# Four chunks turned by VectorE and by DMAs through memory instead of by TensorE, in a two-layer attention and SwiGLU kernel

## The chip, the cores and the metric

The kernel runs on one core of one Trainium2 chip. The metric is the device time of one execution in microseconds (us); the median of the runs counts. Engines are named as in the profile: PE is TensorE, DVE is VectorE, ACT is ScalarE, POOL is GpSimd, SP is SyncE, whose queue issues nearly all transfers here.

## The reference

Two layers of the same two blocks, with the same weights in both, on x of 2048 rows by 448 in float32:

```python
x = x + A(layernorm(x))   # 16 heads of 28; one key and one value head for all
x = x + B(layernorm(x))   # (silu(x @ w_gate) * (x @ w_up)) @ w_down, inner width 1792
x = x + A(layernorm(x))
x = x + B(layernorm(x))

q = (x @ wq) by heads; k = x @ wk; v = x @ wv
A = softmax(q k^T * 28**-0.5) v, heads side by side, @ wo
```

## The kernel before

The 2048 rows are four chunks of 512, numbered c = 0 to 3 in the code and 1 to 4 in the text. A chunk is four tiles of 128 rows by 448. The residual `xres` stays in SBUF. A product needs the normalized chunk turned, with the 448 features on the partitions: four blocks of 128, the last of which holds 64 features twice. `flipped` makes from each turned block a rounded high part `xh` (a ScalarE copy) and a low part `xl` (a VectorE subtraction); of the fourth block the low part lies in the upper half of `xh`, and in the feed-forward the high part of the upper half in `xd`.

There are two ways from rows to a turned chunk, and `norm_steps(c, away)` prepares for either: statistics (`stat`), the scale (`scale`, on POOL), and then for each of four tiles `apply`, which normalizes.

- With `away` false the tiles go to `xn`, and `flip` has TensorE transpose them, 16 transposes of 128x128 into four PSUM banks (line 275), from which `flipped` reads.
- With `away` true each tile is normalized into `sg` (of which there is one buffer, that the feed-forward's SiLU writes too), VectorE transposes it in blocks of 32x32 (`turn`, line 239), and `send` writes the blocks to a tensor `xt` in memory with four DMAs (line 248). `load` brings it back as `raw` with two DMAs (lines 128 and 129), and `cut` calls `flipped` on that. Line 129 reads the last 64 rows and writes them twice, to both halves of the partitions.

The order on each engine's queue is the order in which the program is written down; nothing is reordered. Each engine takes its queue in order and waits at an instruction until its data and buffers are ready.

The stages of a layer are the projections of q, k and v (`Attention.project`, 16 calls, four for each chunk), the scores with softmax and p v, and the feed-forward. The feed-forward goes through the inner width in seven groups of two blocks, and in each group through the four chunks; one block of one chunk is a `unit`. A unit writes in this order: the first half of its gate and up products, the first half of the down product of the unit before, the second half of its own, the second half of the other, and then SiLU, product and rounding of `h`. Between the halves ScalarE copies one column of each bank that was written (`between`, `seen`, line 328); TensorE's next write to that bank comes after that copy.

Work is hung on units by counters: an entry `[n, f]` of `soon` runs at the end of a unit, when its counter, lowered once a unit, is below zero; `mid[gi, c, n]` runs in the middle of that unit; `plan[n, z]` runs in the n-th call of `project`, before (z = 0) or after (z = 1) its product.

- Layer 1's projections turn all four chunks on TensorE. The chunks 1 to 3 that go into the feed-forwards are turned by VectorE and DMAs during the scores.
- Chunk 4 of the feed-forward (`rest`) is normalized at the second unit, and TensorE transposes it in `mid[0, 2, 1]`, two units before the first that multiplies it.
- Layer 2's projections begin inside layer 1's last group (`hand_over(c)`, called when chunk c has got its last addition). Chunk 1 is turned by VectorE and DMAs; chunks 2, 3 and 4 by TensorE, each one call of `project` before the first that needs it (`project` looks ahead in `order`, where the first of a chunk has m = 3).

The first three calls of `project` of layer 2 run at the end of the last unit, the fourth after it, then `flush` (the last down product and its additions), and `finish` runs the other twelve. Each call has ScalarE copy its product from the bank to `stage` (two buffers here) and SP store that to `qd` and `kt`.

Weights of the feed-forward lie in `wgh` and `wgl`, three buffers each (`FG + 1`). During the hand-over these also serve as buffers for `vt`, `wrq` and `q2`.

Of the kernel before, what the change touches and what calls it, by code (L numbers as in the profile page):

```python
# [8 lines left out]
F32 = mybir.dt.float32  # L9
F32R = mybir.dt.float32r  # L10
# [5 lines left out]
P = 128  # L16
# [10 lines left out]
FG = 2  # L27
# [25 lines left out]
def forward(  # L53
# [14 lines left out]
    nc = tc.nc  # L68
# [9 lines left out]
    pers = ctx.enter_context(tc.tile_pool(name="pers", bufs=1))  # L78
    ps = ctx.enter_context(tc.tile_pool(name="ps", bufs=1, space=PSUM))
    dram = ctx.enter_context(tc.tile_pool(name="dram", bufs=1, space=bass.MemoryType.DRAM))  # L80
    wpool = ctx.enter_context(tc.tile_pool(name="wpool", bufs=1))
# [3 lines left out]
    phase, banks, threes, live, turn = ExitStack(), [], [], set(), {}  # L85
# [40 lines left out]
    def rows3(dst, src):  # L126
        n = src.shape[1]
        nc.sync.dma_start(dst[:, 0:3], src[0:384, :].rearrange("(k p) n -> p k n", p=P))
        nc.sync.dma_start(dst[:, 3], src[384:448, :][None].to_broadcast([2, 64, n]))
# [83 lines left out]
    def norm_steps(c, away=False):  # L213


        got = {}
        cs = slice(4 * c, 4 * c + 4)

        def stat(t):
            nc.vector.bn_stats(stats[:, 4 * c + t, :], xres[:, 4 * c + t, :])  # L220
            nc.vector.bn_aggr(mv[:, 4 * c + t, :], stats[:, 4 * c + t, :])

        def scale():
            rstd = pers.tile([P, 4], F32, name="rstd", bufs=2)
            nc.gpsimd.tensor_scalar(rstd, mv[:, cs, 1], 1.0, EPS, ALU.mult, ALU.add)
            nc.gpsimd.tensor_tensor(rstd, rstd, halfn, ALU.pow)
            got["r"] = rstd

        def apply(t):
            if t == 0:  # L230
                got["x"] = pers.tile([P, 4, 512], F32, name="xn")
            got["o"] = (pers.tile([P, 512], F32, name="sg") if away else got["x"][:, t, :])[:, 0:D]
            i, r = xres[:, 4 * c + t, :], got["r"][:, t : t + 1]
            nc.vector.tensor_scalar(got["o"], i, mv[:, 4 * c + t, 0:1], r, ALU.subtract, ALU.mult)
            if not away:
                nc.gpsimd.tensor_copy(got["x"][:, t, D:512], got["o"][:, 384:D])

        def turn(t):
            nc.vector.transpose(side()[:, :, :, t], got["o"].rearrange("p (k s) -> p k s", s=32))

        def side():
            return got["x"].rearrange("p t n -> p (t n)")[:, 0 : 4 * D].rearrange("p (k s t) -> p k s t", s=32, t=4)

        def send():
            turns.append(dram.tile([D, 512], F32, name=f"xt{len(turns)}"))
            got["xt"] = turns[-1]
            for a in range(4):
                nc.sync.dma_start(
                    got["xt"].rearrange("(k r) n -> r k n", r=32)[:, :, P * a : P * a + P],
                    side()[32 * a : 32 * a + 32].rearrange("p k s t -> p k (s t)"),  # L250
                )

        def load():
            got["raw"] = pers.tile([P, 4, 512], F32, name="xn")
            rows3(got["raw"], got["xt"])

        got["load"] = load
        fs = [lambda t=t: stat(t) for t in range(4)] + [scale]
        for t in range(4):
            fs += [lambda t=t: apply(t)] + [lambda t=t: turn(t)] * away  # L260
        return fs + [send] * away, got
# [3 lines left out]
    def cut(got, tiles, ks=range(4), copy=nc.scalar.copy):  # L265

        for k in ks:
            flipped(tiles, k, got["raw"][:, k, :], copy)

    def flip(got, tiles, ks=range(4)):  # L270

        for k in ks:
            pt = bank(wide[-1])[1]
            for t in range(4):
                nc.tensor.transpose(in_turn(pt)[:, t, :], got["x"][:, t, P * k : P * k + P], ident)  # L275
            flipped(tiles, k, pt, nc.scalar.copy)

    def flipped(tiles, k, pt, copy, steps=(0, 1)):

        xh, xl, xd = tiles  # L280
        twice = xd if k == 3 else None
        if 0 in steps and twice is None:
            copy(xh[:, k, :], pt)
        elif 0 in steps:
            copy(xh[0:64, k, :], pt[0:64, :])
            copy(xd[64:128, :], pt[64:128, :])
        if 1 in steps and k < 3:
            nc.vector.tensor_tensor(xl[:, k, :], pt, xh[:, k, :], ALU.subtract)
        elif 1 in steps:
            high = xh[64:128, k, :] if twice is None else xd[64:128, :]  # L290
            nc.vector.tensor_tensor(xh[64:128, k, :], pt[64:128, :], high, ALU.subtract)
# [31 lines left out]
    seen = pers.tile([P, 4], F32, name="seen")  # L323
# [8 lines left out]
    class Attention:  # L332
# [232 lines left out]
        def scores(self, ff):  # L565
            next(switch)
            with tc.tile_pool(name=f"at{self.layer}", bufs=1, reuse_waits="tile") as wp:
# [126 lines left out]
                for c in range(3):  # L694
                    ff.X[c] = xtile(xpool) if c < 2 else None
                    fs, got = norm_steps(c, True)
                    n = NT * (4 * c + 5)
                    for kt, f in enumerate(fs):
                        later[n + kt] = f
                    later[n + 22] = got["load"]  # L700
                    for k in range(4) if c < 2 else ():
                        for z in range(2):
                            later[n + 34 + 2 * k + z] = lambda c=c, got=got, k=k, z=z: flipped(
                                ff.X[c], k, got["raw"][:, k, :], nc.vector.tensor_copy, (z,)
                            )
                ff.norms[2] = got
                last = NT * len(GR)
# [43 lines left out]
    class FeedForward:  # L751
# [68 lines left out]
        def hand_over(self, c):  # L820

            a = self.nxt
            fs, got = norm_steps(c, c == 0)
            for f in fs[:5]:
                f()
            a.pool = self.stage
            a.X[c] = xtile(xpool if c < 2 else self.xbp)

            def ready():
                for f in fs[5:]:  # L830
                    f()
                a.norms[c] = got

            if c == 0:
                self.soon.append([1, lambda: [f() for f in fs[5:]]])
                self.soon.append([2, got["load"]])
                self.soon.append([4, lambda: cut(got, a.X[c])])
                self.soon.append([5, lambda: [a.project() for _ in range(3)]])
            elif c == 1:
                self.soon.append([2, ready])  # L840
            else:
                a.plan[4 * c - 4, 0] = [ready]

        def turned(self, c, ks=range(4)):
            flip(self.norms[c], self.X[c], ks)

        def flush(self):

# [69 lines left out]
        def rest(self, xb):  # L918
            self.stage = xb.enter_context(tc.tile_pool(name=f"stage{self.layer}", bufs=2, reuse_waits="tile"))
            self.xbp = xb.enter_context(tc.tile_pool(name=f"xb{self.layer + 1}", bufs=2, reuse_waits="tile"))  # L920
            xd = xb.enter_context(tc.tile_pool(name=f"xd{self.layer}", bufs=1, reuse_waits="tile"))
            self.xd = [xd.tile([P, 512], F32R, name=f"xd{c}") for c in range(NC)]
            for c in (0, 1):
                dma(self.xd[c][64:128, :], self.X[c][0][0:64, 3, :])
                self.X[c] = (*self.X[c][:2], self.xd[c])
            for c in (2, 3):
                self.X[c] = xtile(self.xbp, self.xd[c])
            cut(self.norms[2], self.X[2])
            third, self.norms[3] = norm_steps(3)
            for f in third[:5]:  # L930
                f()
            self.soon.append([1, lambda: [f() for f in third[5:]]])
            self.mid[0, 2, 1] = [lambda ks=ks: self.turned(3, ks) for ks in ((0, 1), (2, 3))]
            for gi, fs in enumerate(groups):
                if self.layer == 1 and fine is not None and gi in (2, 3):
                    self.verdict(gi == 3)
                    if gi == 3:
                        tc.mark_branch_hint_location("again", engines=(ET.Activation, ET.DVE, ET.Pool, ET.SP, ET.PE))
                for c in range(NC):
                    for n in range(len(fs)):  # L940
                        if gi or c:
                            self.unit(gi, c, n)
                if gi == len(groups) - 2 and self.nxt:
                    self.nxt.w = load_wqkv(xb.enter_context(tc.tile_pool(name="wqkv1", bufs=1, reuse_waits="tile")), None)[1]
            if self.nxt:
                self.nxt.project()
            self.flush()
# [11 lines left out]
    fs, got = norm_steps(0)  # L959
# [28 lines left out]
    for c in range(1, NC):  # L988
        fs, got = norm_steps(c)
# [39 lines left out]
```

## Time and profile before

| | |
|---|---|
| median of 3 runs | 1986.07 us (1986.04 to 1986.16) |
| profiled execution, span | 1984.8 us |
| between the span and the median | 1.3 us |
| PE busy | 1969.2 us (99%) |
| ACT busy | 1278.6 us (64%) |
| DVE busy | 812.1 us (41%) |
| POOL busy | 528.7 us (27%) |
| transposes of line 275 | 144 |
| DMA, mean | 39 GB/s |

Of the profiled execution the page gives the span, from its first instruction to its last; the runs' time is taken around it. A line of a timeline has the start in us from the span's start, the duration, engine and line, what was written from what, the count of instructions run together, and in brackets the idle time before and what ended it. In the chain, which merges pieces, a line is start, duration, engine, tile and line. Lines of waits end with the total, the count and the longest.

### The profile page before, as it was taken

The numbers are of one execution on the slowest core, as the hardware profiler recorded it, in microseconds if no ns is written. First come the engines' busy times: TensorE is split into PE (matmuls) and PEld (weight loads), VectorE is DVE, ScalarE is ACT, GpSimd is POOL, SyncE is SP. The second block draws the span as 40 slices with busy tenths as digits, with TensorE's granted clock in tenths as the row PEclk, the third lists the DMA queues.
The fourth block names the chain that finished last, engine by engine and source line by source line (L and its number), as shares of the span: only waits on it lengthen the run. The fifth ranks groups of instructions, "written<-read, shape, count | busy, mean of one in ns | idle before, by whom it ended". The sixth has DMA issues, their size and how long they took to land. (4 is left out here: it accounts for less than half of the span.)

```text
span 1984.8 us, 44687 instructions
## 1 busy us (share of the span) xinstructions
PE 1969.2 (99%) x18519; PEld 1322.9 (67%) x18519; DVE 812.1 (41%) x1410; ACT 1278.6 (64%) x2140; POOL 528.7 (27%) x571
## 2 busy tenths in 40 slices
PE   9999999999999999999999999999999999999998
PEld 7544545445458999999984444454454789988887
DVE  7444543544434222322554335445454432222222
ACT  4899797997953333333349998979979433333332
POOL 4212111132213233333341221111231232233320
PEclk9999999999999999999999999999999999999999
DMA  5101020121210011100131111102111101011102
GB/s 163 55 23 31 23 51 21 32 58 28 72 33 9 24 32 32 32 24 19 51 107 35 30 31 30 44 12 61 32 55 45 31 17 30 18 31 32 32 1 76
DMA packets 93382, 77.52 MB, mean 39 GB/s; under 512 B 23510, under 2 KB 76374, under 8 KB 93174
## 3 DMA queue, kind: packets, MB, share of 16 engines
q1 hardware_dynamic: 92886, 74.16, 13.5%
q8 instruction: 146, 2.39, 0.5%
q14 instruction: 62, 0.51, 0.1%
q10 hardware_dynamic: 288, 0.46, 0.1%
HBM read 55.06 MB, written 18.74 MB: 37 GB/s over the span
## 5 line engine op out<-in xcount | busy, mean ns | idle before, releaser
L647 PE MATMUL bank<-pt,vsb 128*32 128x512 f32 x4096 | 493.3, 598 | 0.5
L604 PE MATMUL bank<-qstack,keys 32*128 32x512 f32 x1536 | 484.2, 424 | 1.7 <-DVE xres L591 1.7
L604 PE MATMUL three<-qstack,keys 32*128 32x512 f32 x4608 | 461.4, 425 | 1.5 <-DVE vt L538 1.2
L604 PEld LDWEIGHTS three<-qstack,keys 32*128 32x128 f32 x4608 | 254.2, 182 | 295.0 <-ACT pt L617 181.1
L321 PE MATMUL bank<-xh,wgh 64*128 64x512 f32 x1728 | 437.5, 389 | 0.1
L611 ACT ACTIVATE pt<-three 128x1536 f32<-128x1536 f32 x256 | 372.2, 1454 | 0.6 <-ACT pt L617 0.3
L617 ACT ACTIVATE pt<-three 128x1536 f32<-128x1536 f32 x256 | 372.0, 1453 | 0.0
L321 PE MATMUL bank<-xh,wgl 64*128 64x512 f32 x1404 | 363.0, 390 | 0.0
L321 PE MATMUL bank<-wdh,h 64*128 64x448 f32 x1792 | 330.2, 364 | 1.4 <-ACT h L889 1.0
L321 PE MATMUL bank<-xl,wgh 64*128 64x512 f32 x1296 | 328.3, 389 | 0.0
L888 DVE TENSOR_TENSOR sg<-bank,sg 128x512 f32<-128x512 f32 x112 | 77.4, 691 | 497.6 <-ACT sg L887 488.4
L647 PEld LDWEIGHTS bank<-pt,vsb 128*32 128x32 f32 x4096 | 107.1, 109 | 250.2 <-issue 152.6
L613 DVE COPY raw<-bank 128x512 f32<-128x512 f32 x256 | 177.2, 692 | 230.7 <-PE bank L604 228.5
L321 PEld LDWEIGHTS bank<-xh,wgh 64*128 64x128 f32 x1728 | 256.9, 184 | 16.7 <-issue 0.9
L798 POOL TENSOR_TENSOR xres<-stage,xres 128x448 f32<-128x448 f32 x108 | 127.7, 1203 | 499.6 <-ACT stage L797 499.6
L657 DVE TENSOR_TENSOR o<-bank,o 128x512 f32<-128x512 f32 x224 | 154.9, 691 | 241.7 <-PE bank L647 237.1
L321 PEld LDWEIGHTS bank<-wdh,h 64*128 64x128 f32 x1792 | 240.5, 184 | 15.6 <-issue 2.0
L604 PEld LDWEIGHTS bank<-qstack,keys 32*128 32x128 f32 x1536 | 243.8, 183 | 4.6 <-DVE xres L591 3.6
L328 ACT COPY seen<-bank 128x1 f32<-128x1 f32 x664 | 81.0, 163 | 238.9 <-PE bank L321 236.4
L321 PEld LDWEIGHTS bank<-xh,wgl 64*128 64x128 f32 x1404 | 212.1, 184 | 13.8
L321 PE MATMUL bank<-wdl,h 64*128 64x448 f32 x896 | 215.6, 367 | 0.0
L887 ACT ACTIVATE sg<-bank 128x512 f32<-128x512 f32 x112 | 67.3, 601 | 223.2 <-PE bank L321 214.2
(127 smaller groups left out, 2259.3 us busy)
## 6 DMA issues: line engine op xcount, KB each, us to landing
o<-rd SPq DMA_DIRECT2D x32, 256.0 KB
qraw<-qd SPq DMA_DIRECT2D x128, 56.0 KB
qd<-stage SPq DMA_DIRECT2D x30, 224.0 KB
xt<-xn SPq DMA_DIRECT2D x28, 224.0 KB
wdr<-in_B_w_down_dram SPq DMA_DIRECT2D x28, 224.0 KB
xn<-xt SPq DMA_DIRECT2D x7, 768.0 KB
wr<-in_B_w_gate_dram SPq DMA_DIRECT2D x28, 192.0 KB
wr<-in_B_w_up_dram SPq DMA_DIRECT2D x28, 192.0 KB
```

The costliest lines, as they stand in the source:

```text
L321: nc.tensor.matmul(po, a, b, start=start, stop=stop, skip_group_check=True)
L328: nc.scalar.copy(seen[:, i : i + 1], po[:, 0:1])
L604: nc.tensor.matmul(three[:, j, :] if j < 3 else one, k[js, kp, ks], q[js, part, :], start=(z == 0), stop=(z == 2), tile_position=(32 * j, 0),)
L611: nc.scalar.activation(pt, three, AF.Exp, scale=SCALE)
L613: nc.vector.tensor_copy(raw, one)
L617: nc.scalar.activation(pt, three, AF.Exp, scale=SCALE)
L647: nc.tensor.matmul(po[32 * j : 32 * j + 32, :], vsb[:, n % NT, :], pts[n][j], start=(n == 2 * d), stop=(n > 2 * d), skip_group_check=True,)
L657: nc.vector.tensor_tensor(acc, in_turn(po), acc, ALU.add)
L798: nc.gpsimd.tensor_tensor(r, s, r, ALU.add)
L887: nc.scalar.activation(by_tile(sg), in_turn(pg[0]), AF.Silu)
L888: nc.vector.tensor_tensor(by_tile(sg), in_turn(pg[1]), by_tile(sg), ALU.mult)
```

## The change

Chunk 4 of both feed-forwards and chunks 2 to 4 of layer 2's projections go the way of `away=True`. Their transposes on TensorE and the POOL copies that belong to them are gone; for each, VectorE makes four block transposes, SP issues four stores to memory and the loads back, and ScalarE and VectorE cut the parts from SBUF instead of PSUM. `load` has a second form that reads into two buffers taken from the weights' tags, with three DMAs (new lines 262 to 264; the last again writes 64 rows to both halves of the partitions). The hand-over gets an entry of its own for the turn, the load (`fill`) and the cut (`parts`) of each chunk.

```diff
-        def load():
-            got["raw"] = pers.tile([P, 4, 512], F32, name="xn")
-            rows3(got["raw"], got["xt"])
+        def load(spare=None):
+            if spare is None:
+                raw = pers.tile([P, 4, 512], F32, name="xn")
+                rows3(raw, got["xt"])
+                got["raw"] = [raw[:, k, :] for k in range(4)]
+                return
+            two = [
+                wpool.tile([P, 2, 512], F32R, tag=tag, name="xraw", bufs=FG + 1).bitcast(F32) for tag in spare
+            ]
+            nc.sync.dma_start(two[0], got["xt"][0:256, :].rearrange("(k p) n -> p k n", p=P))
+            nc.sync.dma_start(two[1][:, 0, :], got["xt"][256:384, :])
+            nc.sync.dma_start(two[1][:, 1, :], got["xt"][384:448, :][None].to_broadcast([2, 64, 512]))
+            got["raw"] = [half[:, k, :] for half in two for k in range(2)]
...
         def hand_over(self, c):
             a = self.nxt
-            fs, got = norm_steps(c, c == 0)
+            fs, got = norm_steps(c, True)
             for f in fs[:5]:
                 f()
             a.pool = self.stage
             a.X[c] = xtile(xpool if c < 2 else self.xbp)
-
-            def ready():
-                for f in fs[5:]:
-                    f()
-                a.norms[c] = got
-
+            turn = lambda: [f() for f in fs[5:]]
+            fill = lambda: got["load"](("wgl", "wgh") if c < 2 else ("wgl", "wgl"))
+            parts = lambda: cut(got, a.X[c])
+            plan = lambda seen, z, f: a.plan.setdefault((seen, z), []).append(f)
+            if c < 2:
+                self.soon += [[1, turn], [2, fill]]
             if c == 0:
-                self.soon.append([1, lambda: [f() for f in fs[5:]]])
-                self.soon.append([2, got["load"]])
-                self.soon.append([4, lambda: cut(got, a.X[c])])
+                self.soon.append([4, parts])
                 self.soon.append([5, lambda: [a.project() for _ in range(3)]])
             elif c == 1:
-                self.soon.append([2, ready])
+                plan(3, 0, parts)
+            elif c == 2:
+                self.soon.insert(0, [1, turn])
+                plan(4, 1, fill)
+                plan(6, 0, parts)
             else:
-                a.plan[4 * c - 4, 0] = [ready]
+                plan(4, 0, turn)
+                plan(8, 0, fill)
+                plan(10, 0, parts)
...
             cut(self.norms[2], self.X[2])
-            third, self.norms[3] = norm_steps(3)
+            third, got = norm_steps(3, True)
             for f in third[:5]:
                 f()
             self.soon.append([1, lambda: [f() for f in third[5:]]])
-            self.mid[0, 2, 1] = [lambda ks=ks: self.turned(3, ks) for ks in ((0, 1), (2, 3))]
+            self.soon.append([2, got["load"]])
+            self.mid[0, 2, 1] = [lambda ks=ks: cut(got, self.X[3], ks) for ks in ((0, 1), (2, 3))]
```

More of the change, by code (lines that the diff above doesn't have):

```diff
@@ L267, in cut @@
         for k in ks:
-            flipped(tiles, k, got["raw"][:, k, :], copy)
+            flipped(tiles, k, got["raw"][k], copy)
     def flip(got, tiles, ks=range(4)):
@@ L703, in scores @@
                             later[n + 34 + 2 * k + z] = lambda c=c, got=got, k=k, z=z: flipped(
-                                ff.X[c], k, got["raw"][:, k, :], nc.vector.tensor_copy, (z,)
+                                ff.X[c], k, got["raw"][k], nc.vector.tensor_copy, (z,)
                             )
@@ L827, in hand_over @@
             a.X[c] = xtile(xpool if c < 2 else self.xbp)
-            def ready():
-                for f in fs[5:]:
-                    f()
-                a.norms[c] = got
+            turn = lambda: [f() for f in fs[5:]]
[4 more added lines that the diff above has]
+                self.soon += [[1, turn], [2, fill]]
             if c == 0:
-                self.soon.append([1, lambda: [f() for f in fs[5:]]])
-                self.soon.append([2, got["load"]])
-                self.soon.append([4, lambda: cut(got, a.X[c])])
+                self.soon.append([4, parts])
                 self.soon.append([5, lambda: [a.project() for _ in range(3)]])
             elif c == 1:
-                self.soon.append([2, ready])
-            else:
-                a.plan[4 * c - 4, 0] = [ready]
-        def turned(self, c, ks=range(4)):
-            flip(self.norms[c], self.X[c], ks)
+                plan(3, 0, parts)
[3 more added lines that the diff above has]
+                plan(6, 0, parts)
+            else:
+                plan(4, 0, turn)
+                plan(8, 0, fill)
+                plan(10, 0, parts)
         def flush(self):
```

## The prediction

> **What bounds the kernel now.** I read the page first (busy times, chain), then the listing of the transposes' line, then the timeline of each engine in the three places that the change touches, and the order of instructions on each engine's queue.
>
> ```profile
> span 1984.8 us, 44687 instructions
> PE 1969.2 (99%) x18519; PEld 1322.9 (67%) x18519; DVE 812.1 (41%) x1410; ACT 1278.6 (64%) x2140; POOL 528.7 (27%) x571
> PE bank L969 <- POOL ident masks.py:199: 1.9, 1, 1.9
> L275 PE MATMUL bank<-ident,xn x144: 271/273/332, 10.6 to 1604.4; 128*128 128x128 f32 x144
> 1001.19 1.47 PE L275 MATMUL bank<-ident,xn 128*128 128x128 f32 x12
> 1003.55 0.50 PE L301 MATMUL bank<-xh,wh 128*128 128x512 f32 x1
> 1018.29 1.75 PE bank L275 x16
> 1601.22 1.02 PE bank L275 x8
> ```
>
> TensorE is busy for 99% of the span, and its longest single wait is 1.9 us, at the start. So each microsecond taken off its queue is gained, and each in which it waits is lost: nothing later makes up for it. The span is 1984.8 us and the median of the runs 1986.07, so 1.3 us lie around the span; I work in the span's clock and add the differences to the median.
>
> **What leaves TensorE.** Of 144 transposes 64 (layer 1's projections) stay. Gone are 16 for chunk 4 ahead of each feed-forward, in two lots of 8 such as that at 1601.22, 2 x 1.02 = 2.04 us per layer, and 16 for each of chunks 2, 3 and 4 of layer 2's projections: 1.75 us for 3 (1018.29) and the same for 4, and 2.36 us for 2 (1001.19 to the next product at 1003.55, a short wait included). Together 2 x 2.04 + 2 x 1.75 + 2.36 = 9.9 us, the most that there is to gain. The queue order has these 80 gone, so that the change doesn't happen is no case.
>
> **What comes in, priced on the chunk that goes this way already** (chunk 1 of layer 2; rows of DVE, ACT, SP, then the DMA rate in 40 slices of 0.3 us from 976):
>
> ```profile
> 964.57 0.52 DVE L234 TENSOR_SCALAR sg<-xres,mv,rstd 128x448 f32<-128x448 f32 x1
> 969.84 0.98 DVE L239 STREAM_TRANSPOSE xn<-sg 128x448 f32<-128x448 f32 x1
> 970.91 0.60 ACT L887 ACTIVATE sg<-bank 128x512 f32<-128x512 f32 x1 [3.83 <-DVE xn L239]
> 970.85 3.06 SPq L248 DMA_DIRECT2D xt<-xn  x4
> 977.24 0.38 SPq L128 DMA_DIRECT2D xn<-xt  x1
> 977.67 0.51 SPq L129 DMA_DIRECT2D xn<-xt  x1
> GB/s 172 169 14 0 0 0 0 102 96 48 89 259 403 389 416 389 328 143 61 75 55 55 41 55 55 41 55 55 41 55 41 55 55 41 55 0 0 0 0 0
> ```
>
> Normalizing and turning four tiles holds VectorE from 964.57 to 970.82, 6.25 us, and `sg` with it, so the next SiLU waits. SP's four stores follow at once (3.06 us of issue), the load waits for them and issues 6.4 us after the turn's end. Three quarters of it run at about 400 GB/s until about 981.4 (4.2 us after issue). The last quarter (L129, rows 384 to 448 twice, 256 KB) trickles at about 50 GB/s until 986.5, 8.8 us after its issue. So a chunk's first rows are there 10.6 us and its last 15.7 us after the turn. Chunk 1 hides that behind two more units. The feed-forwards' new loads are of this form; those of the hand-over have L264 in place of L129, with the same two-copy destination.
>
> [...]
>
> **Feed-forward, chunk 4 (both layers).** Rows of layer 1; in layer 2 each of them lies 981.4 us later, in the same order.
>
> ```profile
> 611.40 1.78 DVE L234 TENSOR_SCALAR xn<-xres,mv,rstd 128x448 f32<-128x448 f32 x4
> 619.88 0.24 ACT L328 COPY seen<-bank 128x1 f32<-128x1 f32 x2 [0.95 <-PE bank L321]
> 620.41 1.07 ACT L283 CAST xh<-bank 128x512 fp32r<-128x512 f32 x2 [0.29 <-PE bank L275]
> L286 ACT CAST xd<-xn x2: 616/616/617, 597.4 to 1578.8; 64x512 fp32r<-64x512 f32 x2
> 625.81 0.60 ACT L887 ACTIVATE sg<-bank 128x512 f32<-128x512 f32 x1 [1.29 <-PE bank L321]
> 627.16 0.62 ACT L889 CAST h<-sg 128x512 fp32r<-128x512 f32 x1 [0.76 <-DVE sg L888]
> 629.60 0.36 PE L321 MATMUL bank<-wdh,h 64*128 64x448 f32 x1
> ```
>
> The turn keeps its place (611.40), takes 6.25 us instead of 1.78, and ends at 617.65. The load issues at 624.05 and 624.5, its parts land at 628.2 and 633.3. But the copies stand in ScalarE's queue where the trace has 620.41, in the middle of a unit, and behind them stand that unit's `seen` copies, for which the second half of the down product waits (it writes the banks they read), and its SiLU. ScalarE waits until 628.2, copies two (to 629.5), does `seen`, copies the third, and waits for the last quarter until 633.3; its two copies (0.62 each from SBUF) end at 634.55. SiLU to the end of the `h` cast takes 1.97 us (625.81 to 627.78), here about 2.1 since VectorE subtracts first: 636.7. Then the next down product starts, which in the trace started at 629.60: 7.1 us later, with the 2.04 us of transposes already out of it. VectorE's longer turn costs nothing more, as it lies inside that wait. **Both layers: 14.2 us.**
>
> **Projections of layer 2.** SP's queue is the point: each chunk's four stores wait for VectorE and stand ahead of stores of `q` that ScalarE needs done (`stage` has two buffers).
>
> ```profile
> 984.73 0.60 ACT L887 ACTIVATE sg<-bank 128x512 f32<-128x512 f32 x1 [1.96 <-PE bank L321]
> 987.46 2.19 ACT L283 CAST xh<-xn 128x512 fp32r<-128x512 f32 x4
> 996.52 0.69 DVE L892 TENSOR_TENSOR h<-sg,h 128x512 fp32r<-128x512 f32 x1 [0.69 <-ACT h L889]
> 997.07 0.32 SPq L532 DMA_DIRECT2D qd<-stage  x1
> GB/s 0 0 0 0 0 0 0 131 246 287 303 49 0 0 0 0 0 131 279 287 287 66 0 0 0 0 0 147 287 287 180 17 45 2 0 0 0 0 0 0
> 1010.04 0.62 DVE L220 BATCH_NORM_STATS2 stats<-xres 128x6 f32<-128x448 f32 x1
> 1013.59 1.18 POOL L226 TENSOR_TENSOR rstd<-rstd,halfn 128x4 f32<-128x4 f32 x1
> 1014.88 1.79 SPq L406 DMA_DIRECT2D qraw<-qd  x4
> 1009.59 7.77 PE bank L301 x33
> 1020.04 10.03 PE bank L301 x44
> 1032.76 10.03 PE bank L301 x44
> 1033.07 0.31 DVE L435 STREAM_TRANSPOSE flat<-two 128x128 f32<-128x128 f32 x1
> ```
>
> (The rate's slices are 0.25 us from 996: a `q` store is done 1.9 us after issue.)
> Chunk 2's turn now delays the SiLU at 984.73 by 1.8 us, and the tail of that unit by about as much. Chunk 3's turn follows the last `h` (996.52 + 0.69, here about 997.6) and ends at 1003.85. Its stores hold SP until 1006.95, so the store of the first `q` issues then, not at 997.07, and is done at about 1009.5. Only then may ScalarE evict the third `q`; chunk 2's copies (2.2 us) and the fourth eviction follow, to 1012.9, and then `seen`, for which the last down product's second half waits. The fifth projection starts at 1014.5 instead of 1009.59: **+4.9 us**.
>
> Chunk 4's statistics move to 1016.1, its scale is ready at 1020.8 (4.7 us later, as 1010.04 to 1014.77), the turn ends at 1027.1, its stores at 1030.2. Chunk 3's load stands behind them: it issues at 1031.0 to 1031.9, and its last quarter lands 8.8 us later, at 1040.7. ScalarE and VectorE end its copies at 1042.2; the ninth projection, the first that needs chunk 3, ends at 1042.7. In the trace it ended at 1025.05 (the second of the four from 1020.04): **+17.7 us**. Chunk 4's load stands behind the maxima's row store (VectorE, 2.4 us after the copies, 1044.6), two `q` stores and four `qraw` loads (1.8 us): issue at 1047.3 to 1048.2, landed at 1057.0, copied at 1058.3. The thirteenth ends at 1058.8, in the trace at 1037.8 (the second of the four from 1032.76): **+21.0 us**. The last three follow at their old pace. This replaces the two smaller figures, it isn't added to them.
>
> Sum: 14.2 + 21.0 = 35.2, so **2021 us**. Bounds, by other loads of that kind:
>
> ```profile
> 1507.38 0.53 SPq L129 DMA_DIRECT2D xn<-xt  x1
> GB/s 0 17 0 0 0 53 160 180 319 287 238 242 209 135 98 98 82 57 45 82 49 49 49 49 49 49 49 25 0 0 0 0 0 0 0 0 0 0 0 0
> 1051.40 0.53 SPq L383 DMA_DIRECT2D wrk<-kt  x1
> 1057.09 0.63 POOL L139 TENSOR_SCALAR keys<-wrk 128x512 fp32r<-128x512 f32 x1 [5.71 <-DMA wrk<-kt]
> ```
>
> Beside another load L129 took 11.1 us (1507.38 to 1518.5, slices of 0.5 us from 1505); a four-copy load of as many bytes took 5.7. I take 8.8, the same form without company. The last quarter counts once in each feed-forward and twice in the projections (chunks 3 and 4): 4 x 3.1 = 12.4 less or 4 x 2.3 = 9.2 more, 2009 to 2030.
>
> **The rivals.** *All hidden*: each landing comes before ScalarE gets to its copies, and 9.9 us are gained: 1976. It decides at 620.4: the data would have to be there 2.8 us after the turn, where chunk 1 took 15.7. For it speaks only that chunk 1 itself cost no visible wait. *Feed-forward alone pays*: if SP let the `q` stores through and the later loads were in time, the projections gain 1.75 + 1.75 + 2.36 = 5.9, and 14.2 - 5.9 gives 1994; the queue order is against it. *TensorE restarts slowly after each wait*:
>
> ```profile
> L969 PE MATMUL bank<-ident x54: 272/273/474, 1.9 to 9.5; 128*128 128x128 f32 x54
> 1.80:5.00 3.20, 3.11 (x15) 1.00 0.87 245
> ```
>
> In the kernel's first 3.2 us of work (window 1.80 to 5.00: span, TensorE busy and count, granted clock) 15 transposes start, and one takes up to 474 ns; those at 1018.29 start every 0.11 us. So a slow start costs 3.2 - 15 x 0.11 = 1.6 us, though the granted clock reads 1.00. The trace has no later wait over 1.9 us that would show whether it returns; the change makes five of 5 us and more (one per feed-forward, three in the projections): 5 x 1.6 = 8.0, 2029. [...]
>
> **How the numbers follow.** The forecast 0.50 (2021, own range 2009 to 2030), slow restarts 0.30 (2029, up to 2038 with the upper bound), feed-forward alone 0.08, all hidden 0.05, a mix that comes out even 0.02, worse than all of these (other transfers queued behind the trickle on the same engines) 0.05. The range 2005 to 2037 leaves out the last four, under 2 in 10. A measurement of this kernel can tell about 0.2%, 4 us, from no change: faster 0.05, same 0.02, slower 0.93.
>
> **What would show it.** After: ScalarE idle for about 8 us before the SBUF copies near 620 and 1602, ended by the DMA of `xn`; SP waiting for VectorE at the stores before the first `q` store; TensorE waits on ScalarE and VectorE of 5 to 10 us, about 35 to 45 us more in sum than now, and 64 transposes left. Wrong it is if those copies start without a wait, or if the first `q` store still issues right after its eviction.

## The result and the profile after

The changed kernel takes 2040.94 us (median), the kernel before 1986.05 beside it: ratio 1.0274, 95% interval 1.0260 to 1.0289, so 54.9 us slower. The forecast was 2021 us (2005 to 2037): the direction held, the size was 20 us short.

The page of the changed kernel (span, busy time) and its view of waits (total, count, longest) answer to the first fence of the prediction:

```profile
span 2038.6 us, 44571 instructions
PE 1979.6 (97%) x18439; PEld 1262.0 (62%) x18439; DVE 835.7 (41%) x1430; ACT 1273.2 (62%) x2140; POOL 522.6 (26%) x551
PE bank L331 <- ACT seen L338: 21.9, 7, 7.9
PE bank L311 <- ACT xh L293: 12.3, 3, 10.2
PE bank L311 <- DVE xh L301: 5.8, 2, 3.2
PE bank L311 <- DVE vt L548: 2.4, 1, 2.4
L285 PE MATMUL bank<-ident,xn 128*128 128x128 f32 x64 | 8.9, 278 | 0.3
```

The 80 transposes are gone: 64 are left. In their place TensorE waits, 42.4 us in these four rows. PE's busy time has risen by 10.4 us although it has 80 instructions fewer; part of that is work at a granted clock of 0.50, seen below.

To put the loss in its places I measure two stretches between the same two instructions in every kernel. The *seam* goes over layer 1's feed-forward chunk 4, from one SiLU to the SiLU four units later (601.49 to 633.55 before, 601.24 to 641.62 changed). The *projections* go from a SiLU deep in layer 1's feed-forward to SP's first `qd<-sg` store, which follows the last projection. Their two ends, first in the kernel before and then in the changed one:

```profile
903.41 0.60 ACT L887 ACTIVATE sg<-bank 128x512 f32<-128x512 f32 x1 [2.15 <-PE bank L321]
1047.03 0.38 SPq L532 DMA_DIRECT2D qd<-sg  x1
```

```profile
911.47 0.60 ACT L898 ACTIVATE sg<-bank 128x512 f32<-128x512 f32 x1 [1.97 <-PE bank L331]
1091.27 0.38 SPq L542 DMA_DIRECT2D qd<-sg  x1
```

| kernel | seam, us | projections, us | median, us | ratio to before (95%) |
|---|---|---|---|---|
| before | 32.1 | 143.6 | 1986.1 | |
| changed | 40.4 | 179.8 | 2040.9 | 1.0260 to 1.0289 |
| e1, projections alone | 32.1 | 178.8 | 2021.8 | 1.0160 to 1.0194 |
| e2, feed-forwards alone | 40.3 | 143.6 | 2004.6 | 1.0072 to 1.0106 |
| e3, last quarter in two transfers | 39.2 | 170.0 | 2027.2 | 1.0188 to 1.0222 |
| e4, spare transposes, banks moved | 43.1 | 179.1 | 2045.0 | 1.0276 to 1.0310 |
| e5, spare transposes, banks as in the changed kernel | 41.9 | 178.9 | 2043.0 | 1.0268 to 1.0302 |
| e6, four buffers | 40.3 | 177.3 | 2038.8 | 1.0248 to 1.0282 |
| e7, stores in another order | 40.4 | 157.9 | 2020.5 | 1.0157 to 1.0191 |
| e8, e3 and e7 | 39.0 | 149.0 | 2008.6 | 1.0097 to 1.0131 |
| e9, feed-forwards alone, a unit earlier | 30.6 | 144.5 | 1984.9 | 0.9985 to 1.0003 |
| e10, projections' second chunk alone | 32.1 | 143.8 | 1987.1 | 0.9998 to 1.0016 |
| e11, e9 and e10 | 30.6 | 143.6 | 1984.1 | 0.9982 to 1.0000 |
| e12, e8 and e9 | 30.6 | 150.0 | 1992.7 | 1.0019 to 1.0042 |

So the changed kernel loses 8.3 us at the seam, about as much again in layer 2 (8.2), and 36.2 in the projections: 52.7 of the 53.8 us by which the span grew. Stretches of untouched code scatter by about 1 us (e9's projections are those of before).

**The feed-forward waited where the forecast had it wait.** ScalarE's timeline, then TensorE's, in the changed kernel:

```profile
628.59 1.14 ACT L293 CAST xh<-xn 128x512 fp32r<-128x512 f32 x2 [7.93 <-DMA xn<-xt]
634.04 0.62 ACT L295 CAST xh<-xn 64x512 fp32r<-64x512 f32 x1 [3.55 <-DMA xn<-xt]
635.33 0.60 ACT L898 ACTIVATE sg<-bank 128x512 f32<-128x512 f32 x1
641.62 0.60 ACT L898 ACTIVATE sg<-bank 128x512 f32<-128x512 f32 x1 [1.96 <-PE bank L331]
629.96 0.74 PE L331 MATMUL bank<-wdh,h 64*128 64x448 f32 x2 [5.80 <-ACT seen L338]
```

The two landings are at 628.6 and 634.0 (forecast 628.2 and 633.3), ScalarE idle for 7.93 us as foretold.

**In the projections SP's queue sets the order.** SP's timeline, then ScalarE's:

```profile
1011.77 3.04 SPq L248 DMA_DIRECT2D xt<-xn  x4
1014.85 1.21 SPq L542 DMA_DIRECT2D qd<-stage  x1
1016.11 1.31 SPq L545 DMA_DIRECT2D kt<-stage  x1
1040.97 1.18 SPq L542 DMA_DIRECT2D qd<-stage  x1
1042.19 1.29 SPq L545 DMA_DIRECT2D kt<-stage  x1
1044.55 0.53 SPq L264 DMA_DIRECT2D xraw<-xt  x1
1063.30 1.59 SPq L416 DMA_DIRECT2D qraw<-qd  x4
1065.88 0.53 SPq L264 DMA_DIRECT2D xraw<-xt  x1
1006.36 0.59 ACT L541 COPY stage<-bank 128x512 f32<-128x512 f32 x1 [1.66 <-PE bank L311]
1019.80 0.59 ACT L541 COPY stage<-bank 128x512 f32<-128x512 f32 x1 [10.36 <-DMA kt<-stage]
1055.59 0.62 ACT L293 CAST xh<-xraw 128x512 fp32r<-128x512 f32 x1 [5.36 <-DMA xraw<-xt]
1074.89 0.62 ACT L293 CAST xh<-xraw 128x512 fp32r<-128x512 f32 x1 [4.33 <-DMA xraw<-xt]
1079.07 0.59 ACT L541 COPY stage<-bank 128x512 f32<-128x512 f32 x1 [2.10 <-DMA kt<-stage]
```

The first projection is copied to `stage` at 1006.36, but its store issues at 1014.85, behind the four stores of the turned chunk, which had waited for VectorE. The third copy, which needs the buffer back, comes at 1019.80 after 10.36 us of waiting. Chunk 3's load and chunk 4's each stand behind more such stores and waits.

### The profile page after: what moved, and what is told of

Its sections match the earlier page's. It is cut to its first block, busy times and chain, and to the rows that moved or that the text cites. A ratio compares the mean times of both kernels' runs of the same rounds, so it can differ in the third digit from the quotient of the medians.

```text
span 2038.6 us, 44571 instructions
## 1 busy us (share of the span) xinstructions
PE 1979.6 (97%) x18439; PEld 1262.0 (62%) x18439; DVE 835.7 (41%) x1430; ACT 1273.2 (62%) x2140; POOL 522.6 (26%) x551
## 5 line engine op out<-in xcount | busy, mean ns | idle before, releaser
L331 PE MATMUL bank<-xh,wgh 64*128 64x512 f32 x1728 | 341.1, 390 | 1.8 <-ACT seen L338 0.9
L331 PE MATMUL bank<-wdh,h 64*128 64x448 f32 x1792 | 299.5, 368 | 22.7 <-ACT seen L338 21.0
L331 PE MATMUL bank<-xh,wgl 64*128 64x512 f32 x1404 | 298.6, 391 | 0.0
L623 DVE COPY raw<-bank 128x512 f32<-128x512 f32 x256 | 177.3, 693 | 230.9 <-PE bank L614 228.6
L331 PE MATMUL bank<-xl,wgh 64*128 64x512 f32 x1296 | 255.5, 390 | 0.0
L338 ACT COPY seen<-bank 128x1 f32<-128x1 f32 x664 | 75.7, 164 | 242.7 <-PE bank L331 241.9
L331 PEld LDWEIGHTS bank<-wdh,h 64*128 64x128 f32 x1792 | 171.4, 186 | 51.4 <-ACT seen L338 23.4
L626 ACT ACTIVATE pt<-bank 128x512 f32<-128x512 f32 x256 | 151.3, 591 | 64.3 <-PE bank L614 64.1
L696 POOL TENSOR_TENSOR o<-o 128x512 f32<-128x512 f32 x32 | 41.2, 1287 | 583.5 <-DMA o<-rd 484.8
L331 PEld LDWEIGHTS bank<-xh,wgh 64*128 64x128 f32 x1728 | 164.0, 185 | 34.9 <-DVE xh L301 1.8
```

Of the source, the lines that this page charges most:

```text
L331: nc.tensor.matmul(po, a, b, start=start, stop=stop, skip_group_check=True)
L338: nc.scalar.copy(seen[:, i : i + 1], po[:, 0:1])
L623: nc.vector.tensor_copy(raw, one)
L626: nc.scalar.activation(pt1, one, AF.Exp, scale=SCALE)
```

## The experiments

### Which part costs what (e1, e2)

e1 puts the feed-forwards' chunk back on TensorE, e2 the projections' chunks.

```diff
 # e1: rest, against the changed kernel
-third, got = norm_steps(3, True)
+third, self.norms[3] = norm_steps(3)
 ...
 # e2: hand_over
-fs, got = norm_steps(c, True)
+fs, got = norm_steps(c, c == 0)
 ...
```

> Chunk 4 ahead of both feed-forwards is turned on TensorE again; the projections of layer 2 stay changed. Theory (the feed-forwards cost 8.2 us each, as the SiLU of the unit after the copies lies 8.1 to 8.3 us later): 2041 - 16.5 = 2024.5 us. The recorded sum had 7.1 each, so 2027 by it. Rival (most of the loss beyond the forecast arises in the feed-forwards, by the clock or the weights' loads behind the new load): 2012 or less.

> The projections of layer 2 are as before the change; the feed-forwards' chunk 4 stays changed. Theory: 1986 + 2 x 8.2 = 2002.5 us, so the projections carry 38 of the 55 us. Recorded sum: 2000. Rival (the two parts feed each other, since a late first stage moves the second's transfers): the two single prices of e1 and e2 add up to less than 50 us of the 55.

Measured: 2021.77 and 2004.64 us, against 1986.42 before. The projections alone cost 35.4 us, the feed-forwards alone 18.2; together 53.6 of 54.9, so the parts add. In the prediction they were 21.0 and 14.2. By far the larger miss, 14.4 of 18.4 us, is in the projections.

### The last quarter of a load (e3)

The transfer that reads 64 rows and writes them to both halves becomes two transfers of 64 partitions, with the same bytes.

```diff
-nc.sync.dma_start(two[1][:, 1, :], got["xt"][384:448, :][None].to_broadcast([2, 64, 512]))
+for h in (0, 64):
+    nc.sync.dma_start(two[1][h : h + 64, 1, :], got["xt"][384:448, :])
```

> The change, but the last quarter of every new load is written by two DMAs of 64 partitions each instead of one DMA whose destination begins with two copies. Theory (that form runs on few engines, and ScalarE waits for its trickle): the fourth copy follows the third without the 3.5 us wait in each feed-forward (4 us each), and the last quarters of chunks 3 and 4 in the projections land 5 to 7 us earlier: 8 + 12 = 20 us less, 2021 us. Rival (the last quarter is late because of the transfers queued beside it, not because of its form): within 4 us of 2041.

Measured: 2027.23 us, 13.7 less than the changed kernel. The trickle is in the path, but worth less than the theory asked for. ScalarE's timeline, TensorE's, and a window of TensorE (window, busy, then the columns of the other engines, granted clock, DMA share and GB/s):

```profile
1048.31 1.77 ACT L296 CAST xh<-xraw 128x512 fp32r<-128x512 f32 x3 [15.37 <-DMA xraw<-xt]
1050.50 0.62 ACT L296 CAST xh<-xraw 128x512 fp32r<-128x512 f32 x1 [0.43 <-DMA xraw<-xt]
632.41 0.60 ACT L901 ACTIVATE sg<-bank 128x512 f32<-128x512 f32 x1
640.53 0.60 ACT L901 ACTIVATE sg<-bank 128x512 f32<-128x512 f32 x1 [1.95 <-PE bank L334]
630.72 0.74 PE L334 MATMUL bank<-wdh,h 64*128 64x448 f32 x2 [6.46 <-ACT seen L341]
632.00:634.00 2.00, 2.00 (x14) 1.65 (x12) 1.38 (x2) 1.12 (x3) 0.00 (x0) 0.50 0.56 148
```

In the projections the wait for the last quarter falls from 5.36 us to 0.43, and the stretch by 9.8 us. At the seam the SiLU comes 2.9 us earlier (632.41 for 635.33), but the next one only 1.1 (640.53 for 641.62): the step between them is 8.12 us where the changed kernel has 6.29. TensorE starts at 630.72 after a wait, runs with a granted clock of 0.50 and doesn't wait again before the second SiLU. In the changed kernel the same slow work (629.96 to 633.65, a granted clock of 0.50 in 630.0 to 633.5) lay beside ScalarE's wait of 3.55 us for the last quarter, which TensorE then waited for too (0.57 us at 636.08), and cost nothing; with that wait gone it is late next. That is where the gain missing at the seam went.

### The clock after a wait (e4, e5)

Spare transposes of the identity are written into the long waits, so that TensorE rests less; what they write is not read. In e5 the order in which PSUM banks are given out is as in the changed kernel, in e4 it had moved.

```diff
+def fill_in(cands, n):
+    idle = bank(cands)[1]
+    for _ in range(n):
+        nc.tensor.transpose(idle[:, 0:P], ident, ident)
 ...   # and the calls, in the long waits
```

> The change, but TensorE makes spare transposes of the identity in the long waits (48 in each feed-forward, 62 before the last down product's second half, 86 and 14 ahead of the ninth and thirteenth projections, 44 and 34 inside these, ahead of the matmuls that need the last quarter), so that its waits are shorter than 3 us; what it waits for is the same. Theory (the granted clock of 0.5 after each long wait delays the work that follows): the clock stays above 0.95 there and the time falls by 6 to 10 us, to 2031 to 2035. Rival (the slow stretches lie inside time that is waited anyway): 2039 to 2043.

> As the run with spare transposes, but these use the next free bank without moving the order in which banks are handed out (in the first of the two, the unit after them had to wait 4.2 us for a bank whose SiLU stood behind the copies). Theory (time lost to the slow clock, 1 us in each feed-forward and 5 in the projections): 2034 us, the clock above 0.95 in all the long waits. Rival (the slow stretches lie inside time that is waited anyway): 2039 to 2042.

Measured: 2044.95 and 2042.96 us, 4.0 and 2.0 more than the changed kernel, and 1 to 2 us above what the rivals allowed. Since e4 also moved the banks it decides nothing by itself. Windows of the changed kernel, then of e5 (the third number from the end is the granted clock), and a row of TensorE's timeline in e5:

```profile
1020.00:1030.00 10.00, 6.67 (x22) 5.25 (x23) 8.76 (x17) 5.74 (x14) 6.58 (x12) 0.51 0.48 140
1040.00:1050.00 10.00, 0.76 (x2) 0.32 (x2) 0.78 (x2) 1.43 (x3) 0.00 (x0) 0.67 0.73 194
```

```profile
1020.00:1030.00 10.00, 7.32 (x54) 6.42 (x53) 7.08 (x12) 4.13 (x12) 5.13 (x9) 0.91 0.55 165
1040.00:1050.00 10.00, 9.89 (x86) 9.40 (x84) 0.78 (x1) 0.00 (x0) 0.00 (x0) 1.00 0.67 164
1028.37 0.80 PE L321 MATMUL bank<-xh,wh 128*128 128x512 f32 x1 [1.38 <-DVE xres L816]
```

The clock does fall with the long waits (0.51 and 0.67 in the changed kernel's windows), and the spare work holds it up in them (0.91 and 1.00 in e5's), yet the time doesn't fall: from the first copy to `stage` to the last projection the stretch is 0.9 us shorter, and the seam 1.5 us longer. So slow restarts are real, but most of the slow work behind the long waits has slack beside it in the changed kernel. e5 is not a full test: waits of 1.4 to 2.5 us are left in it, and behind three of them (the row above is the first) matmuls again start 0.43 us apart instead of 0.23, for about 3 us. Where the changed kernel's trace shows the slow clock in the path, at the end of the projections, it is worth 2.4 us (below); that is a small part of the missing 20, and e7 gives back 20.4 by the order alone. Nor does a slow stretch here need a wait as long as those: in the row above it follows a wait of 1.38 us, with one of 1.30 shortly before it. Whether the path feels it is another matter; e3 and the end of the projections show that.

### A buffer or the queue (e6)

```diff
-tc.tile_pool(name=f"stage{self.layer}", bufs=2, reuse_waits="tile")
+tc.tile_pool(name=f"stage{self.layer}", bufs=4 if self.nxt else 2, reuse_waits="tile")
```

> The change, with four stage buffers instead of two in the hand-over, so that ScalarE evicts the third projection without waiting for the first one's store. Theory that this wait (10.4 us at 1009.4) is the root in the projections: the fifth projection starts 8 us earlier and the time falls by 10 to 14 us, 2027 to 2031. Rival (SP's queue is the root, since VectorE's next work waits for the loads behind the same stores, and chunk 3's load stands behind chunk 4's turn): the fifth projection starts earlier, the ninth doesn't, and the time falls by 2 to 5 us, 2036 to 2039.

Measured: 2038.76 us, 2.2 less, as the rival has it. ScalarE's third copy and its next wait, then SP's queue:

```profile
1010.95 0.59 ACT L541 COPY stage<-bank 128x512 f32<-128x512 f32 x1 [1.91 <-PE bank L311]
1019.45 0.53 ACT L807 COPY stage<-bank 128x448 f32<-128x448 f32 x1 [4.29 <-DMA kt<-stage]
1014.46 1.21 SPq L542 DMA_DIRECT2D qd<-stage  x1
1020.32 0.69 SPq L400 DMA_DIRECT2D few<-kt  x1
```

The 10.36 us wait of the third copy is gone (it is at 1010.95), but the first store still issues at 1014.46, and the fifth to need a buffer, the copy of the last down product (L807), waits for the same stores. TensorE waits 7.63 us ahead of the fifth projection, which starts at 1024.27 instead of 1026.06, not 8 us sooner; chunk 3's last load issues at 1042.76 for 1044.55 (the execution as a whole is 0.4 us earlier there). ScalarE's wait, its longest for a buffer, was for the most part a symptom.

### The order in SP's queue (e7, e8)

The four stores of chunks 3 and 4 go behind the stores of q that are ready earlier; VectorE's blocks stay where they are. e8 has the edit of e3 as well.

```diff
-turn = lambda: [f() for f in fs[5:]]
+turn = lambda: [f() for f in (fs[5:] if c < 2 else fs[5:-1])]
 ...
+plan(3, 1, fs[-1])   # chunk 3: behind the fourth q
 ...
+plan(5, 1, fs[-1])   # chunk 4: behind the sixth q
```

> The change, with the stores of the turned chunks 3 and 4 moved in SP's queue: chunk 3's stand behind the store of the fourth projection, chunk 4's behind that of the sixth, and so behind chunk 3's load. Nothing else is moved. Theory (SP's order carries most of the projections' 35 us): the first store of q issues within 1 us of its eviction, chunk 3's load issues near 1030 instead of 1043.6, chunk 4's near 1048 instead of 1064.9, and the time falls by 22 to 30 us, 2011 to 2019. Rival (the trickle and the slow clock carry it): within 8 us of 2041.

> The order of e7 and the spread last quarters of e3 together. Theory (two causes in a chain, each shortens it): e3 alone gave 13.7 us; with the order 8 us more in the projections and the same 6 in the feed-forwards, 1999 to 2005. If the two overlap (with the order mended the loads come in time and the trickle no longer matters there), 2005 to 2013.

Measured: 2020.52 us for e7, 20.4 less than the changed kernel (a little short of what the theory asked), and 2008.61 for e8, 32.3 less. SP's queue and ScalarE's copies in e7:

```profile
1007.92 0.34 SPq L542 DMA_DIRECT2D qd<-stage  x1
1016.00 3.41 SPq L248 DMA_DIRECT2D xt<-xn  x4
1023.54 0.38 SPq L262 DMA_DIRECT2D xraw<-xt  x1
1012.42 0.59 ACT L541 COPY stage<-bank 128x512 f32<-128x512 f32 x1 [2.03 <-DMA kt<-stage]
1034.27 0.62 ACT L293 CAST xh<-xraw 128x512 fp32r<-128x512 f32 x1 [4.47 <-DMA xraw<-xt]
```

The first store issues 0.6 us after its copy starts, in 0.34 us instead of 1.21; the third copy waits 2.03 us instead of 10.36. Chunk 3's own stores issue 4.2 us later (1016.00 for 1011.77), and yet its last quarter is used 21.3 us sooner (1034.27 for 1055.59; the execution as a whole is 1.0 us later there), as the load no longer has chunk 4's turn ahead of it. The order alone gives back 21.9 of the 36.2 us, order and spread 30.8; 5.4 us stay. Alone they give 21.9 and 9.8, so in the projections they add to within the scatter of 1 us. e8's time lies in the range for an overlap (2005 to 2013), but that of the sum counted on 22 us or more from the order.

### Enough work in between (e9, e10, e11)

e9 has the feed-forwards' chunk alone, with three things moved: it is turned and loaded one unit earlier, the last quarter comes in two transfers, and the copies stand one step later in their unit, behind its `seen` copies. e10 has only the projections' second chunk, which has the feed-forward's last units and three projections before it. e11 is both edits in one.

```diff
 # e9, rest
-self.soon.append([1, lambda: [f() for f in third[5:]]])
-self.soon.append([2, got["load"]])
+self.soon.append([0, lambda: [f() for f in third[5:]]])
+self.soon.append([1, got["load"]])
-self.mid[0, 2, 1] = [lambda ks=ks: cut(got, self.X[3], ks) for ks in ((0, 1), (2, 3))]
+self.mid[0, 2, 1] = [lambda: None] + [lambda ks=ks: cut(got, self.X[3], ks) for ks in ((0, 1), (2, 3))]
 ...
 # e10, hand_over
-fs, got = norm_steps(c, True)
+fs, got = norm_steps(c, c < 2)
 ...
```

> The projections of layer 2 are the kernel before's. The fourth chunk ahead of both feed-forwards is turned by VectorE and memory, but one unit earlier: its turn behind the first unit, its load behind the second, the last quarter by two transfers of 64 partitions each, and its copies cut one step later in the unit that cuts them. Theory (the method is free where the work in hand is longer than the way through memory): in the changed kernel the load was issued at 624.05 and had landed at 633.3, with the last quarter spread at about 630; one unit of some 7 us earlier it lands before its copies are wanted, TensorE waits for nothing, the transposes of the chunk are saved (by the prediction 2 to 3 us for each feed-forward), and the unit beside the blocks loses about 1 us of VectorE. 1981 to 1986 us, no longer slower than before. Rival (a transfer through memory costs the path something wherever it is put, since its copies and SiLUs share ScalarE and VectorE): a wait of 2 us or more stays in each feed-forward, 1988 us or more.

> Only the second chunk of layer 2's projections is turned by VectorE and memory; the feed-forward's fourth chunk and the projections' third and fourth are turned on TensorE, as in the kernel before. Theory (the price lies in the length of the way against the work between, and the second chunk has the feed-forward's last units and the first three projections before it): TensorE waits for nothing new, it saves 16 transposes (about 2 us), and the blocks on VectorE take about 1 us from the unit they lie beside, as the first chunk's do: 1984 to 1987 us, no difference that counts. Rival (each chunk so turned costs its share of the projections' 35 us, 12 us): 1990 us or more.

> The two kernels above in one: fourth chunk ahead of each feed-forward one unit earlier with the last quarter in two transfers, and the second chunk of layer 2's projections by VectorE and memory, the third and fourth on TensorE. Theory: the two places do not meet, and what each of the two saves or costs adds up, to within 2 us. If both are covered, 1979 to 1986 us, the best of all kernels here and at or below the kernel before. Rival (the traffic through SyncE's queue and the raw buffers, shared with the stores of the feed-forward, delays other work): 1988 us or more.

Measured: 1984.91, 1987.09 and 1984.09 us, against 1986.19 before: each interval reaches 1, so none of the three can be told from the kernel before. The theories' ranges hold to 0.1 us, and the rivals (1988 us or more, 1990 or more) fell. ScalarE's timeline in e9, two rows of SP's between:

```profile
610.53 0.60 ACT L897 ACTIVATE sg<-bank 128x512 f32<-128x512 f32 x1 [4.48 <-DVE xn L239]
616.82 0.38 SPq L256 DMA_DIRECT2D xn<-xt  x1
617.24 1.13 SPq L258 DMA_DIRECT2D xn<-xt  x2
622.08 1.66 ACT L296 CAST xh<-xn 128x512 fp32r<-128x512 f32 x3
623.65 0.62 ACT L298 CAST xh<-xn 64x512 fp32r<-64x512 f32 x1
631.27 0.60 ACT L897 ACTIVATE sg<-bank 128x512 f32<-128x512 f32 x1 [1.95 <-PE bank L334]
```

The same load, issued at 616.82 instead of 623.94, is there when its copies are taken up: no wait stands at 622.08, nor at 623.65, where the last quarter is used. No run moves the chunk by the unit alone; by an estimate from the prediction's row (8.8 us after issue) the last quarter would then have come at about 626.0 and ScalarE waited some 2 us, and the two transfers alone gave 1.2 us at the seam (e3). VectorE's blocks show only as the 4.48 us of ScalarE's idle time before a SiLU. The seam is 1.5 us shorter than with transposes, of the 2.04 that they took. e10's chunk, too, is there in time (its copies, like the first, follow without a wait), and its stretch is that of before to 0.2 us: of the 2.36 us of transposes most goes to the unit beside the blocks, whose two SiLUs lie 9.16 us apart (from 980.34 to 989.50) instead of 7.29.

### All five chunks, mended (e12)

The edits of e8 and e9 in one: chunk 4 ahead of each of the two feed-forwards, and chunks 2 to 4 of the projections.

> All five chunks go through VectorE and memory as in the changed kernel, with three things moved: the feed-forwards' fourth chunk one unit earlier (as in the run of that alone), the last quarter of each load in two transfers, and the stores of the projections' third and fourth chunks behind the stores of q (as in the run of both). From the traces, a stretch over the projections, between the same two instructions, takes 143.6 us before, 179.8 in the changed kernel and 149.0 with order and spread; a feed-forward's seam takes 32.1 us before, 40.4 changed, 39.0 spread and 30.6 one unit earlier. Theory (the places are independent and their terms add): 1986.2 + 5.4 - 2 x 1.5 = 1988.6, at most 3 us to either side, which leaves about 2.5 us lost of the 54.9. Rival (the places share SyncE's queue and the clock, and what one gives the other takes): 1993 us or more.

Measured: 1992.69 us, ratio 1.0030 (1.0019 to 1.0042): 6.5 us lost, 1.1 above what the theory allowed and 0.3 below the rival. So it is undecided between them, but 48 of the 54.9 us are back. Where the theory missed shows in two places: the projections take 150.0 us (149.0 in e8), and in layer 2 the copies wait:

```profile
1605.18 0.38 SPq L256 DMA_DIRECT2D xn<-xt  x1
1610.57 1.66 ACT L296 CAST xh<-xn 128x512 fp32r<-128x512 f32 x3 [1.39 <-DMA xn<-xt]
```

Layer 2's seam is 31.8 us, 1.2 more than layer 1's. There the load issues 7.6 us after the chunk's stores (at 1597.61); in e9 it was 6.3, and the same copies waited 0.23 us. So the cover is just enough, and 1 us of delay in the way shows; what caused the delay is open. No kernel with chunks 3 and 4 through memory came level with the one before.

## Why the prediction was wrong in size

**Held.** Every wait was named at its place: ScalarE's 8 us at the feed-forward (7.93), TensorE's waits in sum (42.4 us in the rows shown, 35 to 45 forecast), SP's stores ahead of the first q store, the loads of chunks 3 and 4 as what ends last, 64 transposes left. *All hidden* and *feed-forward alone pays* fell in the changed kernel; the first comes true where the cover is long enough (e9 to e11), but then gives no more than the scatter: 2.1 us in e11, of the 6.4 that its transposes took. The time came out where *worse than all of these* (0.05) had it; no run tests that case's reason, other transfers behind the trickle, by itself.

**Failed: the size of the projections' term,** 36.2 us for 21.0. In the prediction's own clock (8.06 us taken off, by which layer 1's feed-forward is later) its steps missed as follows; a quarter counts as landed where its copy starts:

| step | forecast | found | late by then |
|---|---|---|---|
| fifth projection starts | 1014.5 | 1018.0 | 3.5 |
| chunk 3's last load issues | 1031.9 | 1036.5 | 4.6 |
| its last quarter lands | 1040.7 | 1047.5 | 6.8 |
| chunk 4's last load issues | 1048.2 | 1057.8 | 9.6 |
| its last quarter lands | 1057.0 | 1066.8 | 9.8 |
| end of the projections | +21.0 | +36.2 | 15.2 |

- *The q store, "done at about 1009.5",* 2.5 us after its issue. Alone such a store took 1.9. Right behind four block stores its issue took 1.21 us instead of 0.32, the `kt` store that the prediction left out another 1.31, and the buffer was free 4.95 us after the first issue. This makes 1.9 of the 3.5 us. The rest is the second half of the last down product, 3.0 us from 1023.06 to the fifth projection at a granted clock of 0.50, where the forecast had 1.6 with the copy before it (in e5 it takes 3.0 too, with 0.20 us from two matmuls to the next two where the changed kernel has 0.38, and a wait of 1.38 us for a bank). The same pair of stores stands again ahead of chunk 3's load (1040.97, 1042.19). e7 took this away, and the issue of the first store fell back to 0.34.
- *The last quarter, "the same form without company".* It has company: 11.0 us from issue to use for chunk 3 (forecast 8.8) and 9.0 for chunk 4. The bound with company, 11.1, stood in the prediction; the likelier value was chosen on the wrong side.
- *Chunk 4's load behind a row store and the* `qraw` *loads.* It also stood behind more waits in that queue: `qraw` could issue only at 1063.30. This 2.8 us was not in the sum.
- *"The last three follow at their old pace."* From the landing to the end it took 5.4 us more. TensorE's start of the fourteenth projection, and a window of TensorE (window, busy, granted clock, DMA share and GB/s):

```profile
1079.40 0.80 PE L311 MATMUL bank<-xh,wh 128*128 128x512 f32 x1 [2.39 <-DVE vt L548]
1078.00:1082.00 4.00, 2.60 (x6) 0.50 0.44 130
```

  It waits 2.39 us for a bank that VectorE reads (`vt`) behind its subtraction and the maxima of the chunk just landed (1075.54 to 1078.59). Then that projection takes 4.86 us, where it took 2.50 before, as its matmuls start 0.43 us apart instead of 0.23. These are 4.8 of the 5.4 us, and TensorE doesn't wait again before the last projection's end. ScalarE's waits for stores (2.10 us at 1079.07 and 1.28 after it) hold up nothing there.

**The feed-forward's term** was 7.1 us each and is 8.3 by the trace, 9.1 by e2. In the clock of the kernel before (0.25 us added, by which the SiLU at 601.24 is earlier) the copy of the last quarter starts at 634.29 for 633.3, 0.9 us of it because the trickle took 9.7 us from issue to use instead of 8.8, and the next down product starts at 637.70 for 636.7. That is 1.0 of the 1.2 us missing by the trace; the rest is not separated.

**The rival of slow restarts,** at 0.30, would have come nearest (2029, up to 2038), but mostly for a wrong reason: the effect exists (a granted clock of 0.50, matmuls 0.43 us apart instead of 0.23), and the trace shows it in the path for 2.4 us at the end of the projections, but five times 1.6 us is not shown.

**The lesson on the range.** It took the trickle alone as unknown, in one direction more than the other. The steps of a chain through one queue were priced by rows from an emptier queue; the errors, up to 5.4 us each, all went in the same direction, and they added. Such a chain needs its bounds at each link, not one for all.

## What to carry to other kernels

Work taken off the bounding engine is a gain only where its replacement is done before that engine asks for it: compare the length of the new way with the work in between, at each place by itself, before counting what was removed (the same chunk cost 8 to 9 us or nothing, after it was turned one unit of 7 us earlier, loaded without the slow form and copied a step later). In a queue that is taken in order, a transfer that waits for another engine holds up all that stands behind it: put it behind what is ready sooner, even if it then starts later (21.9 us here). A long wait may be only where the lateness shows: more buffers moved it to the next user and gave back 2.5 us of 36.

## What was not expected of the hardware

A store of `q` right behind four block stores took 1.2 us to issue (1.21 at 1014.85, 1.18 at 1040.97) where one without them took 0.3 (0.32 before, 0.34 in e7). In the changed kernel the granted clock read 0.50 to 0.52 behind TensorE's waits of 5.80 us (at 629.96), 7.88 (1023.06), 10.22 (1049.24) and 3.23 (1056.98), from 1 us behind one of 1.78 (1069.56), and at 1079.40 behind waits of 2.57 and 2.39 us with two matmuls between them; the work behind ran slowly for 3 to 7 us. In e5, windows with transposes of the identity in place of the wait read 0.91 and 1.00. And the transfer to two copies of 64 rows used 9 to 11 us for 256 KB that as two transfers were there almost with the rest. In the kernel before, the tail of such a transfer ran at 50 GB/s with a DMA share of 0.13 (982.0 to 986.5), where the stretch with the other three quarters (979.3 to 981.1) had 364 GB/s and 0.97. That the form is what is slow, e3 shows: with the same bytes the wait falls from 5.36 us to 0.43.
